# First pair: x ahead of the weights, weight conversions behind each step's work, unread products on TensorE

## The chip, the cores and the metric

One core of one Trainium2 chip. The metric is the device time of one execution in microseconds (us), a few executions per kernel. The rounds of the experiments ran on three chips, each time with the kernel before beside them (median 2079.8 to 2081.2 us). A time is about 1.8 us more than the span of the same execution in its trace. Where a ratio is given with an interval, it is the mean time of one kernel's fast runs over that of the kernel before in the same rounds, so it is not quite the ratio of the medians quoted beside it; the interval is a 95% one.

In the views PE is TensorE, PEld its weight loads, DVE VectorE, ACT ScalarE, POOL GpSimd and SP SyncE; a q behind a name means its sequencer, which waits and issues. The granted clock is the share of full speed that TensorE was given. A landing is the time from a transfer's issue to the arrival of its data. The views count each product twice: three products stand as x6.

## The reference, cut to what matters

```python
x: (8, 3008, 256) f32;  w_in: (256, 2048);  w_out: (2048, 256)   # float64 in memory, read as pairs of int32
X = np.fft.fft(x, axis=1)
X = np.fft.fft(X, axis=2).real
h = X.reshape(24064, 256) @ w_in
g = h * np.clip(h + 3.0, 0.0, 6.0) / 6.0
return g @ w_out
```

The weights arrive in double precision. The kernel converts them to float32 with integer operations while the first x is being transformed.

## The kernel before: the parts concerned

Work is done in batch "pairs"; all the trouble is in the first. x comes in 8 chunks, each as a forward half and a "partner" half, the mirrored rows, which are gathered with an indirect DMA. A fold adds the two (two large operations on GpSimd, then two large and one 8-element operation on VectorE), stage 1 multiplies by the DFT table on TensorE, ScalarE copies the result to z, and z is stored.

```python
def load_x(pr, c):                                   # all on GpSimd's queue; PR = 94 rows
    nc.gpsimd.dma_start(out=xt[:, 0:n, :], in_=rows[...])                    # forward
    nc.gpsimd.indirect_dma_start(out=xr[:]..., in_=x_r, in_offset=...IX...)  # partners
...
narrow_pair(0); use_pair(0)
for c in range(NXC):                                 # window A
    fold(first, c, 0, nc.gpsimd)
    fold(first, c, 1, nc.vector)
    if c + 3 < NXC:
        load_x(first, c + 3)
    if c in (2, 5):
        narrow_pair((c + 1) // 3)                    # conversion: VectorE, ScalarE, GpSimd
    for i in range(XC // 2):
        stage1(first, c, i)
    ...load_w...; if c in (2, 5): use_pair((c + 1) // 3)
load_g(...); narrow_pair(3); stage2 ...; use_pair(3) # window B
# window C: the MLP steps; pairs 4 to 7 are converted AHEAD of steps 0, 1, 3 and 5
```

A conversion of a pair of weight blocks is 5 operations of VectorE, 3 of ScalarE and a last multiplication for each of two blocks, then 4 products and 8 small ones on TensorE (x8 and x16 in the views) for an "in" pair or sums on GpSimd for an "out" pair.

## Time and profile before

Median 2081.8 us (2078.97 to 2082.96). The span is the sum of four stretches, which are used throughout. They were read from the timeline: A ends with the last stage-1 product of the first pair, B with the first hidden s on VectorE, C with the seventh second-layer step.

| stretch, before | us | what runs in it |
|---|---|---|
| A | 84.1 | loads, 8 folds, stage 1, conversion of pairs 0 to 2 |
| B | 22.8 | z out and back in, pair 3, stage 2 |
| C | 80.2 | 7 MLP steps, pairs 4 to 7 |
| rest | 1891.5 | steady MLP, TensorE full |

The rest is TensorE-bound and untouched, so a change in the time is a change in A + B + C. The lines that carry this are in the prediction below. One view was looked at before predicting but not used as it should have been, the table of DMA issues of the first 200 us. Its columns are what is moved, queue and operation, count, size and, last, the median us from issue to landing:

```profile
xt<-in_x_dram POOLq DMA_DIRECT2D x8, 376.0 KB, 10.2
...
xt<-in_x_dram,IX POOLq DMA_INDIRECT x9, 13.8
```

A forward load takes 10.2 us to land and a gather of partners, 94 rows, 13.8 us. The prediction works with 5 us for x.

### The profile page before, as it was taken

The page shows a single profiled execution, that of the slowest core. Times are in us where ns is not written, and L with a number is a line of the kernel's source. Part 1 is how long each engine was busy: PE and PEld are TensorE (multiplying, and loading weights), DVE is VectorE, ACT ScalarE, POOL GpSimd, SP SyncE. Part 2 cuts the span into 40 slices and gives each one's busy share as a digit, 9 for nine tenths or more (in the row PEclk, how much of TensorE's full clock was granted, in tenths as well). Part 3 has the DMA queues.
Part 4 walks back from the last instruction along what each step waited for, and adds up shares of the span by engine and source line. Part 5 has one row for each costly group of instructions (what it writes and reads, how often), then busy time and mean ns, then how long its engine had stood idle before and what let it go on. Part 6 is the DMA issues. An engine that isn't in the chain of part 4 may idle for free.

```text
span 2078.6 us, 28133 instructions
## 1 busy us (share of the span) xinstructions
PE 1974.6 (95%) x9136; PEld 1692.0 (81%) x9136; DVE 1456.9 (70%) x2714; ACT 706.1 (34%) x1205; POOL 1496.1 (72%) x1662
## 2 busy tenths in 40 slices
PE   4468999999999999999999999999999999999997
PEld 1246888888888888888888888888888888888886
DVE  5366676776777677677677677677777777777775
ACT  2344333333333333333333333333333323333332
POOL 6248777877667887788667778778766766766765
PEclk7688999999999999999999999999999999999999
DMA  6420211221110122212111112211110011011000
GB/s 188 142 86 15 57 49 34 50 47 33 29 31 23 44 51 51 51 33 54 29 21 34 43 34 48 51 43 47 31 36 11 17 23 21 18 24 21 16 16 18
DMA packets 158161, 86.81 MB, mean 42 GB/s; under 512 B 132512, under 2 KB 145056, under 8 KB 158016
## 3 DMA queue, kind: packets, MB, share of 16 engines
q1 hardware_dynamic: 129856, 60.28, 12.7%
q0 software_dynamic: 28160, 24.73, 4.5%
q8 instruction: 74, 1.21, 0.3%
q14 instruction: 71, 0.58, 0.1%
HBM read 47.65 MB, written 37.22 MB: 41 GB/s over the span
## 4 chain that ended last, share of the span: by engine, by line
PE 91%; DVE 4%; DMA 2%; ACT 1%; issue 1%; POOL 1%; SPq 0%; DVEq 0%; POOLq 0%; ACTq 0%
PE acc L320 53%; PE v L266 16%; PE u L266 15%; PE ps L193 2%; PE ps L221 2%; PE wps L446 1%; PE ps L237 1%; DVE a L298 1%; DMA st<-in_moe_w_in_dram 1%; ACT t L295 1%; DVE u L279 0%; DVE ex L406 0%; DVE s L271 0%; PE wns L451 0%; DMA g<-zd 0%
## 5 line engine op out<-in xcount | busy, mean ns | idle before, releaser
L310 POOL TENSOR_TENSOR c<-a 128x512 f32<-128x512 f32 (+1 forms) x384 | 479.2, 1248 | 406.7 <-DVE a L298 258.7
L320 PE MATMUL acc<-c,G 128*128 128x256 f32 (+1 forms) x3072 | 714.1, 375 | 0.0
L320 PEld LDWEIGHTS acc<-c,G 128*128 128x128 f32 x3072 | 579.3, 191 | 73.8 <-POOL c L310 0.2
L295 ACT ACTIVATE t<-u,half 128x512 f32<-128x512 f32 (+2 forms) x416 | 272.3, 655 | 1074.8 <-DVE u L279 1063.2
L271 DVE SCALAR_TENSOR_TENSOR s<-qn,WN,u 128x256 f32<-128x256 f32 x768 | 334.4, 477 | 392.2 <-PE u L266 391.9
L320 PE MATMUL acc<-a,G 128*128 128x256 f32 (+1 forms) x2304 | 553.6, 377 | 0.0
L320 PEld LDWEIGHTS acc<-a,G 128*128 128x128 f32 x2304 | 436.8, 191 | 57.3
L266 PE MATMUL v<-q,W 128*128 128x256 f32 x1536 | 398.8, 382 | 17.9 <-DVE a L298 17.9
L266 PE MATMUL u<-q,W 128*128 128x256 f32 x1536 | 394.5, 379 | 0.0
L266 PEld LDWEIGHTS v<-q,W 128*128 128x128 f32 x1536 | 291.3, 191 | 64.3 <-issue 21.9
L266 PEld LDWEIGHTS u<-q,W 128*128 128x128 f32 x1536 | 287.4, 190 | 65.3 <-issue 20.9
L298 DVE SCALAR_TENSOR_TENSOR a<-t,u 128x512 f32<-128x512 f32 (+2 forms) x416 | 265.9, 646 | 105.3 <-ACT t L295 101.0
L310 POOL TENSOR_TENSOR c<-a,c 128x256 f32<-128x256 f32 (+1 forms) x384 | 275.0, 716 | 30.1
L310 POOL TENSOR_TENSOR c<-c,a 128x256 f32<-128x256 f32 (+1 forms) x384 | 275.0, 716 | 30.1
L279 DVE TENSOR_TENSOR u<-s,v 128x512 f32<-128x512 f32 (+1 forms) x384 | 263.0, 685 | 42.6 <-PE v L266 2.5
L295 ACT ACTIVATE t<-v,half 128x512 f32<-128x512 f32 (+1 forms) x384 | 257.0, 669 | 5.3 <-DVE v L285 4.4
L285 DVE TENSOR_TENSOR v<-v,s 128x512 f32<-128x512 f32 (+1 forms) x384 | 257.7, 671 | 1.1
L298 DVE SCALAR_TENSOR_TENSOR a<-t,v 128x512 f32<-128x512 f32 (+1 forms) x416 | 255.1, 619 | 0.1
L310 POOL TENSOR_TENSOR r<-w,e 128x256 f32<-128x256 f32 (+1 forms) x96 | 92.3, 982 | 3.8
L193 PE MATMUL ps<-y,F 94*96 94x512 f32 x120 | 67.0, 656 | 26.2 <-DVE y L159 20.1
L326 ACT ACTIVATE e<-acc 128x512 f32<-128x512 f32 (+1 forms) x192 | 87.0, 543 | 2.9 <-PE acc L320 2.8
L346 DVE STREAM_TRANSPOSE o<-r 128x256 f32<-128x256 f32 (+1 forms) x192 | 72.4, 415 | 6.5 <-POOL r L310 6.4
(70 smaller groups left out, 826.7 us busy)
## 6 DMA issues: line engine op xcount, KB each, us to landing
out_dram<-o SPq DMA_DIRECT2D x736, 32.0 KB, 1.6
zd<-z SPq DMA_DIRECT2D x32, 384.0 KB, 3.0
g<-zd SPq DMA_DIRECT2D x48, 256.0 KB, 4.2
xt<-in_x_dram POOLq DMA_DIRECT2D x28, 376.0 KB, 3.9
st<-in_moe_w_in_dram SPq DMA_DIRECT2D x8, 512.0 KB, 4.4
st<-in_moe_w_out_dram SPq DMA_DIRECT2D x8, 512.0 KB, 5.7
T<-in_c_stage_dram SPq DMA_DIRECT2D x12, 128.0 KB, 7.2
xt<-in_x_dram POOLq DMA_DIRECT2D x4, 282.0 KB, 3.4
```

Source lines behind the costliest of these rows:

```text
L193: nc.tensor.matmul(ps[0:PZ], F[0:PR, 0:PZ], y[:, 2 * i:2 * i + 2, :], start=True, stop=True)
L221: nc.tensor.matmul(ps[:, blk, 2 * u:2 * u + 2], g[:, kk, blk * P:(blk + 1) * P], T[:, :, gr, blk, kk], start=True, stop=True)
L266: nc.tensor.matmul(ps[:, i], W1[:, blk, f * P:(f + 1) * P], q[:, blk, of:of + KC], start=True, stop=True)
L271: nc.vector.scalar_tensor_tensor(s[:, i].rearrange("p k n -> p (k n)"), qn[:, of * N2:(of + KC) * N2], WN[:, f:f + 1], u[:, i].rearrange(" ...
L279: nc.vector.tensor_tensor(u[:, :, 0:ns], s[:, :, 0:ns], v[:, :, 0:ns], op=AL.add)
L285: nc.vector.tensor_tensor(v[:, :, 0:nm], v[:, :, 0:nm], s[:, :, 0:nm], op=AL.subtract)
L295: nc.scalar.activation(t, h, AF.Relu, bias=half[:], scale=scale)
L298: nc.vector.scalar_tensor_tensor(dst, t, 1.0, h, op0=AL.min, op1=AL.mult)
L310: nc.gpsimd.tensor_tensor(out, in0, in1, op=AL.add)
L320: nc.tensor.matmul(ch.acc[i // 2][:, i % 2, 0:ch.n], G[:, i, fc, :], mv, start=(fc == 0 and i % 2 == 0), stop=(fc == NF - 1), skip_group_c ...
L326: nc.scalar.mul(ch.e[:, k:i + 1, 0:ch.n], ch.acc[i // 2][:, 0:i + 1 - k, 0:ch.n], 1.0 / WS)
L346: nc.vector.transpose(o[:, 0:n // DH, h], ch.r[:, m, h, 0:n].rearrange("p (j i) -> p j i", i=DH))
```

## The change

Its intent: get x and the folds through without a weight conversion between them; convert pairs 1 to 7 later, behind work that TensorE already has; fill TensorE's waits for x with products that nobody reads, to keep its clock up (granted clock 0.71 in A and 0.64 in B before). The core of the diff, cut:

```diff
+        nr, eng = (PR + 2, nc.sync) if pr.p == 0 else (PR, nc.gpsimd)     # forward x: 96 rows, SyncE
+        eng.dma_start(out=xt[0:nr, 0:n, :], in_=rows[...])
...
-        eng = nc.vector if j < 6 else nc.gpsimd          # last multiplication of a conversion
+        eng = nc.vector if j < 2 else nc.gpsimd
...
-        nc.scalar.mul(g[5], g[5], -1.0)                  # sign moved into finish()
...
     narrow_pair(0)
+    keep_awake(8)                                        # unread 128x128x512 products
     use_pair(0)
     for c in range(NXC):
         fold(first, c, 0, nc.gpsimd)
+        if c + 3 < NXC:
+            load_partners(first, c + 3)                  # gather, still 94 rows, GpSimd
         fold(first, c, 1, nc.vector)
-        if c + 3 < NXC:
-            load_x(first, c + 3)
-        if c in (2, 5):
-            narrow_pair((c + 1) // 3)
         for i in range(XC // 2):
             stage1(first, c, i)
+        if c + 3 < NXC:
+            load_forward(first, c + 3)
+        keep_awake(3)
...
+    narrow_pair(1); use_pair(1); keep_awake(5)
     load_g(first, 0); load_g(first, 1); load_t(1)
-    narrow_pair(3)
+    narrow_pair(2); use_pair(2)
     stage2 ...
-    use_pair(3)
...                                                      # MLP steps: pairs 3 to 7
-            for i, t in enumerate((0, 1, 3, 5)):         # ahead of step t
+            for i, t in enumerate((0, 1, 1, 3, 4)):      # behind step t
```

More of the change, by code (lines that the diff above doesn't have):

```diff
@@ L47 @@
 NK1 = (N1 + 1) // 2
-PROD = ("P1", "P2", "-P4", "P5", "P7", "P6", "P3")
+PROD = ("P1", "P2", "-P4", "P5", "P7", "-P6", "P3")
 @with_exitstack
@@ L116, in __init__ @@
             self.p = p
-            self.x, self.y, self.z = {}, {}, {}
+            self.x, self.xr, self.y, self.z = {}, {}, {}, {}
             self.zd = None
@@ L125, in x_tile, with load_forward, load_partners @@
             pool, tag = ((apool, "a"), (cpool, "c"), (spool, "t"))[(i >= 8) + (i >= 11)]
-        return pool.tile([PR, XC, D], F32, tag=tag, name="xt")
+        return pool.tile([PR + 2, XC, D], F32, tag=tag, name="xt")
     def load_x(pr, c):
-        xt, xr = x_tile(pr, 2 * c), x_tile(pr, 2 * c + 1)
-        rows = x_pn[pr.p * PR:(pr.p + 1) * PR]
+        load_forward(pr, c)
+        load_partners(pr, c)
+    def load_forward(pr, c):
+        xt = x_tile(pr, 2 * c)
+        nr, eng = (PR + 2, nc.sync) if pr.p == 0 else (PR, nc.gpsimd)
+        rows = x_pn[pr.p * PR:pr.p * PR + nr]
         n = XC if c < NXC - 1 else XC - 1
-        nc.gpsimd.dma_start(out=xt[:, 0:n, :], in_=rows[:, c * XC + 1:c * XC + 1 + n, :])
+        eng.dma_start(out=xt[0:nr, 0:n, :], in_=rows[:, c * XC + 1:c * XC + 1 + n, :])
         if n < XC:
-            nc.gpsimd.dma_start(out=xt[:, n:XC, :], in_=rows[:, 0:1, :])
+            eng.dma_start(out=xt[0:nr, n:XC, :], in_=rows[:, 0:1, :])
+        pr.x[c] = xt
+    def load_partners(pr, c):
+        xr = x_tile(pr, 2 * c + 1)
+        pr.xr[c] = xr
         i = pr.p * NXC + c
         nc.gpsimd.indirect_dma_start(
-            out=xr[:].rearrange("p n d -> p (n d)"), out_offset=None, in_=x_r,
+            out=xr[0:PR].rearrange("p n d -> p (n d)"), out_offset=None, in_=x_r,
             in_offset=bass.IndirectOffsetOnAxis(ap=IX[:, i:i + 1], axis=0),
         )
-        pr.x[c] = xt, xr
     def fold(pr, c, part, eng):
-        xt, xr = pr.x[c]
+        xt, xr = pr.x[c][0:PR], pr.xr[c][0:PR]
         n = XC if c < NXC - 1 else XC - 1
@@ L165, in fold @@
             eng.tensor_copy(y[:, n, 0:P + 1:P], xt[:, n, 0:P + 1:P])
-        del pr.x[c]
+        del pr.x[c], pr.xr[c]
     starting = [True]
@@ L335, in finish @@
         add(rn[:, 0, 0], e[:, 0], e[:, 1])
-        add(wn[:, 0], e[:, 0], e[:, 5])
+        nc.gpsimd.tensor_tensor(wn[:, 0], e[:, 0], e[:, 5], op=AL.subtract)
         add(wn[:, 1:3], wn[:, 0:1].to_broadcast([P, 2, n]), e[:, 4:2:-1])
@@ L472, with keep_awake @@
     nc.vector.memset(ones[:], 1.0)
+    def keep_awake(n):
+        ps = ps_h.tile([P, 2 * TB], F32, tag="uv", name="awake")
+        for i in range(n):
+            nc.tensor.matmul(ps[:], ones[:], W0[:], start=True, stop=True)
+    W0 = spool.tile([P, 2 * TB], F32, tag="s", name="W0")
+    nc.vector.memset(W0[:], 0.0)
     narrow_pair(0)
+    keep_awake(8)
     use_pair(0)
@@ L476 @@
         fold(first, c, 0, nc.gpsimd)
+        if c + 3 < NXC:
+            load_partners(first, c + 3)
         fold(first, c, 1, nc.vector)
-        if c + 3 < NXC:
-            load_x(first, c + 3)
-        if c in (2, 5):
-            narrow_pair((c + 1) // 3)
         for i in range(XC // 2):
             stage1(first, c, i)
-        for j in {0: (2, 3), 2: (4,), 3: (5,), 5: (6,), 6: (7,), 7: (8, 9)}.get(c, ()):
-            load_w(j)
+        if c + 3 < NXC:
+            load_forward(first, c + 3)
+        keep_awake(3)
         if c == 4:
             load_t(0)
-        if c in (2, 5):
-            use_pair((c + 1) // 3)
+            load_w(2)
+        if c == 5:
+            load_w(3)
+            load_w(4)
+    narrow_pair(1)
+    use_pair(1)
+    keep_awake(5)
+    for j in (5, 6):
+        load_w(j)
     load_g(first, 0)
@@ L492 @@
     load_t(1)
-    narrow_pair(3)
+    narrow_pair(2)
+    use_pair(2)
+    for j in (7, 8):
+        load_w(j)
     for i in range(2):
@@ L503 @@
     NST = 2 * NF
+    after = {}
     def beside(p):
@@ L512, in beside @@
         if p == 0:
-            for i, t in enumerate((0, 1, 3, 5)):
-                for j in (10, 11, 12, 13, 14, 15)[2 * i:2 * i + 2]:
-                    put(t, load_w, j)
-                if i + 2 < NG:
-                    put(t, load_t, i + 2)
-                put(t, narrow_pair, 4 + i)
-                put(t, use_pair, 4 + i)
+            for i, t in enumerate((0, 1, 1, 3, 4)):
+                after.setdefault(t, []).extend([(narrow_pair, (3 + i,)), (use_pair, (3 + i,))])
+                for j in range(9 + 2 * i, min(11 + 2 * i, 16)):
+                    after[t].append((load_w, (j,)))
+            for gr in range(2, NG):
+                after.setdefault(gr - 1, []).append((load_t, (gr,)))
             put(NF - 1, close_w)
@@ L573 @@
         mlp2(*chunk(s))
+        for f, a in after.get(s, ()):
+            f(*a)
         if fc == NF - 1:
```

## The prediction

> **What bounds the kernel now.** I read the page's slices first, then busy time in four windows, then the chain that ended last within the first 190 us, then each engine's timeline there.
>
> ```profile
> PE   4468999999999999999999999999999999999997
> PEclk7688999999999999999999999999999999999999
> ```
>
> Each digit is 52 us. TensorE is short of work only in the first three or four slices, and the granted clock is low only there.
>
> ```profile
> 0.00:84.10 84.10, 38.15 (x88) 16.43 (x88) 46.49 (x76) 26.48 (x44) 41.17 (x41) 0.71 0.58 163
> 84.10:106.90 22.80, 11.46 (x48) 8.58 (x49) 3.33 (x7) 7.80 (x13) 3.57 (x3) 0.64 0.59 153
> 106.90:187.00 80.10, 53.95 (x199) 41.30 (x198) 53.57 (x94) 34.94 (x58) 47.71 (x52) 0.81 0.19 56
> 187.00:2078.60 1891.60, 1871.07 (x8805) 1625.69 (x8803) 1353.55 (x2538) 636.84 (x1090) 1403.65 (x1567) 1.00 0.15 34
> ```
>
> Columns: window, length, busy us of PE, PEld, DVE, ACT, POOL, clock, DMA share, GB/s. After 187.0 TensorE is busy 1871 of 1892 us; the change leaves that part alone. So the span is "end of the seventh second-layer step (186.9)" plus a constant, and the question is when that step ends. Call the three earlier windows A (x, folds, stage 1), B (way to the first hidden step) and C (first seven MLP steps, among which weights are still converted).
>
> In A, the chain of waits shows the cause:
>
> ```profile
> 24.03 0.59 ACT z L194
> 24.64 0.34 SPq L196
> 25.02 0.43 SPq L378
> 25.49 13.89 DMA st<-in_moe_w_in_dram
> ...
> 57.99 5.61 DMA st<-in_moe_w_out_dram
> ...
> 84.12 0.59 ACT z L194
> 84.72 3.00 DMA zd<-z
> 87.79 0.64 SPq L206
> 88.48 6.82 DMA g<-zd
> ```
>
> Weight loads stand between the folds: 13.9 and 5.6 us of the chain are a weight block landing, because VectorE converts it ahead of the next fold in program order, while x waits behind the same transfers:
>
> ```profile
> 31.47 1.88 POOL L139 DMA_INDIRECT xt<-in_x_dram,IX  x1 [0.30 <-issue]
> 39.78 1.50 POOL L151 TENSOR_TENSOR xt<-xt 94x508 f32<-94x508 f32 x1 [6.43 <-DMA xt<-in_x_dram,IX]
> ```
>
> In C, conversions cost TensorE 4 to 9 us each:
>
> ```profile
> 119.88 3.97 PE L446 MATMUL wps<-st,C 128*128 128x512 f32 x4 [8.62 <-POOL st L409]
> ...
> 145.47 2.05 PE L266 MATMUL v<-q,W 128*128 128x256 f32 x4 [5.88 <-DVE a L298]
> ```
>
> [...] clock 0.50 in 80:100, 1.00 later; the 128x512 product of L237 is 1.50 us in the cold chain piece (99.19) and 0.87 us in the warm one (207.84). [...] a 0.68 us conversion (L406) took 3.63 us at 44.30 beside GpSimd's folds.
>
> **The change part by part.** A: x forward moves from GpSimd's queue to SyncE's; partners stay on GpSimd, issued straight after its fold; six of eight weight loads, and pairs 1 to 3, leave the loop. GpSimd's 5.04 us per chunk (23.31 less 18.27) loses 0.6 to 0.9 of issue. In return TensorE gets 8 unread products ahead of weight pair 0, 3 after each chunk, 5 after pair 1.
>
> - The zeros are ready some 0.4 us after the ones (10.2), so at 10.6. Eight products at 1.71 cold, 0.86 warm; I estimate 3 cold (in the before, the clock rose 3.4 us after the first product) and 5 warm: 9.4, to 20.0.
> - Pair 0 on PE, warm: 4 x 0.86 + 1.7 (wns) = 5.1, to 25.2. Before it was done at 22.0, so this start is 3 us later.
> - Per chunk 2 stage-1 and 3 unread products, 5 x 0.86 = 4.3 us warm. Beside it: GpSimd 2.35 fold + 2.2 indirect issue = 4.5, but it starts at about 12 and has no partner to issue after chunk 4; x three chunks ahead needs z copy 0.7, issue 0.8, landing about 5, fold 2.35, y 1.4, stage 1 1.7 = 12 per 3 chunks, 4.0 each. So PE's 4.3 sets it, narrowly.
> - Last stage 1: 25.2 + 7 x 4.3 + 2.2 = 57.5, against 84.1. Gain 26.6.
>
> B: Before, 22.8 us. z to g still takes 11.3 (84.1 to 95.4), so g is there at 68.8. But ScalarE's order puts pair 1's conversion behind the last z copy (58.1): 4.35 for six activations (84.60 to 88.95), then 0.7 VectorE and 1.3 GpSimd, 64.6. PE's first product of it can go at 62.3; with a clock probably lost, pair 1 ends near 70.5. Unread 5: 4.3, stage 2 to 77. Pair 2's activations stand behind WN's copy (70.5): GpSimd's second product ends 7.0 later (134.28 to 141.29 in the before), G needs 3.0, then m 1.05: 81.5; ps3 and qn about 2: first hidden s at 83.5 against 106.9. B is 26.0, so 3.2 lost.
>
> C: one hidden step on VectorE is 3.7 (106.89 to 110.58). An "in" pair, from VectorE's start to wns end, is 14.7 (114.27 to 128.99). An "out" pair is 9.9 from ScalarE's start to G (134.28 to 144.2), and no longer has the sign change that held ScalarE to 144.0, worth about 1.9.
>
> - Three hidden steps, 0.8 added for a cold start: 95.4. Second-layer step 0 runs inside.
> - Pair 3: 110.1. Hidden step 3 (1.1 + 3.7): 114.9. Pair 4: 129.6. Pair 5's activations stand behind pair 4's W copies: G at 139.6; step 2 ends 143.3 cold.
> - Stage 2, hidden 5, step 3: 1.0 + 1.9 + 3.0 = 149.2. Pair 6 starts at 149.1 on VectorE, G 159.4, step 4 at 163, step 5 at 167.9. Pair 7 starts 159.3, G 169.7; GpSimd's y folds 2.75 and combine 2.75: 175.2. Step 6 ends 175.9.
>
> C is 92.4 against 80.0: one pair more (five, not four), 12.4 lost. Sum: 26.6 - 3.2 - 12.4 = 11.0 gained. 2081.8 - 11.0 = 2070.8, so 2071.
>
> **Rivals.**
> 1. *The unread products become the bound and never warm the clock.* Cold they are 1.71 each: 8.6 per chunk, stage 1 ending near 95, later than before. For: in the before the clock dropped at 25[...]. Against: the unread ones are full 128 x 128 products without gaps. It would make 2095 to 2110.
> 2. *DMA replaces the weights as the limit.* A chunk moves 0.38 MB in twice and 0.38 MB out; in 4.3 us that is 266 GB/s, while the four 20 us stretches of the before reach 109 to 190 and 80:100 reaches 211. For: that peak. Against: partners run up to three chunks ahead, and slices of the before reach 300 and more. If chunks take 5 us, A ends near 62.5 and the time is 2076.
> 3. *The gain of A is kept whole.* If B and C cost no more than before, 2055. Against: five conversions in series are counted from the program order, and each has one engine's queue behind it.
> 4. *A is eaten entirely*: with pair 1 and 2 serial and cold, C 7 us longer than I have it, 2079 to 2082.
>
> **Range and chances.** The hand count has some 40 terms, several decided by about 1 us of slack; I put plus or minus 12: 2058 to 2083, 2071 the middle. 2% is 41.6 us, which would need step 6 at 145, before my sum has even begun pair 6: 0.03. Slower by 2% needs rival 1 and more: 0.01. Within 2%: 0.96.
>
> **What would show it.** In the after: unread products of 0.86 us at clock 1.0 from about 15 on; first stage 1 at 25, last near 57, chunk spacing 4.3 with PE, not x, ending the waits; no weight load in the chain before 55. In B, PE idle on GpSimd's conversion and m, not on g. In C, PE gaps of 6 to 7 us before pairs 3 and 4 and waits on G before steps 2 and 4; PE continuous from near 176. Wrong if chunks wait for x (rival 2), if the clock reads 0.5 in 25:57 (rival 1), or if pairs 3 to 7 cost TensorE less than 12 us each over its own work.

## The result, and the profile after

Median 2089.57 us (2088.61 to 2093.95), against 2082.3 in the same rounds: ratio 1.0042, interval 1.0024 to 1.0061. That is within 2%, as given the highest chance, but above the predicted range of 2058 to 2083 and on the other side of before: the kernel lost 0.4% where 0.5% was to be gained.

The page's slices (52 us each) of the changed kernel:

```profile
PE   6768999999999999999999999999999999999997
PEclk9978999999999999999999999999999999999999
```

The unread products do what they were put in for: the first two slices were 4 4 busy at clock 7 6 and are now 6 7 at 9 9. The time did not follow. The same four stretches, as windows (columns as in the prediction):

```profile
0.00:71.70 71.70, 51.74 (x123) 22.87 (x124) 35.68 (x57) 15.55 (x25) 32.30 (x28) 0.93 0.60 172
71.70:97.80 26.10, 18.30 (x63) 10.28 (x63) 7.83 (x13) 12.81 (x22) 8.98 (x9) 0.91 0.67 186
97.80:195.40 97.60, 66.79 (x224) 44.86 (x224) 60.40 (x104) 39.33 (x64) 49.49 (x52) 0.78 0.15 46
195.40:2086.90 1891.50, 1870.94 (x8805) 1625.67 (x8803) 1354.11 (x2538) 636.77 (x1090) 1403.51 (x1569) 1.00 0.15 34
```

| stretch | before | predicted | measured | change predicted | change measured |
|---|---|---|---|---|---|
| A | 84.1 | 57.5 | 71.7 | -26.6 | -12.4 |
| B | 22.8 | 26.0 | 26.1 | +3.2 | +3.3 |
| C | 80.2 | 92.4 | 97.6 | +12.4 | +17.4 |
| sum | | | | -11.0 | +8.3 |

B is right, the rest is untouched as expected. A gave 14.2 us too little and C cost 5 us more. (The prediction took 80.0 for C of before.)

In A, the chain of waits (start, us, what) no longer has a weight landing before 61, but it has this:

```profile
2.59 8.91 DMA xt<-in_x_dram
11.54 10.59 issue
22.17 0.70 POOL xt L161
...
25.78 3.15 DVE y L169
...
43.56 6.95 DMA xt<-in_x_dram
...
51.46 3.14 DVE y L169
```

x itself is the first thing on the chain; then comes a stretch of 10.6 us for which the chain names nobody. GpSimd's timeline (start, us, engine, line, operation, and in brackets the idle time before it and its releaser) names it:

```profile
3.84 1.69 POOL L150 DMA_INDIRECT xt<-in_x_dram,IX  x1 [3.39 <-DVE IX L473]
...
22.17 1.25 POOL L161 TENSOR_TENSOR xt<-xt 94x508 f32<-94x508 f32 x1 [12.94 <-DMA xt<-in_x_dram,IX]
...
42.48 1.25 POOL L161 TENSOR_TENSOR xt<-xt 94x508 f32<-94x508 f32 x1 [7.13 <-DMA xt<-in_x_dram]
...
59.25 1.26 POOL L161 TENSOR_TENSOR xt<-xt 94x508 f32<-94x508 f32 x1 [4.70 <-DMA xt<-in_x_dram,IX]
```

The gather issued at 3.84 holds the first fold until 22.17; the prediction had the folds begin at about 12. And from the fold of chunk 0 at 22.17 to that of chunk 3 at 42.48 are 20.3 us, for three chunks. What ends the wait at 42.48 is not a gather (a gather carries IX) but the forward load. SyncE issues it only behind the store of chunk 0's z:

```profile
33.35 0.32 SPq L206 DMA_DIRECT2D zd<-z  x1
33.71 0.44 SPq L141 DMA_DIRECT2D xt<-in_x_dram  x1
```

By the semaphore times in the trace, chunk 3's gather had landed at 37.8 and its forward load landed at 42.3, 8.6 us after its issue. The forward load also came last for chunks 4 and 7, the gather for chunk 6 (the fold at 59.25). The view of the tile over the same stretch, with the count, then the least, median and greatest duration in ns, and its last line, which here holds the gathers alone, gives two more numbers:

```profile
L169 DVE TENSOR_TENSOR y<-xt x8: 161/166/3220, 25.7 to 67.9; 94x8 f32<-94x8 f32 x7, 94x6 f32<-94x6 f32 x1
...
DMA to landing us min/median/max: 12.4/15.8/18.3
```

A gather lands after a median of 15.8 us. And an operation on 8 elements, 0.17 us in the median, takes 3.2 us three times (two of them on the chain, at 25.78 and 51.46). So two suspects for A: the landing of x, gathers and the forward loads beside them, and something that holds VectorE. For C, two more: five conversions in series, and the clock (0.78 against 0.81 before).

### The profile page after: what moved, and what is told of

It is laid out like the page before. It is cut to its first block, busy times and chain, and to the rows that moved or that the text cites. A ratio compares the mean times of both kernels' runs of the same rounds, so it can differ in the third digit from the quotient of the medians.

```text
span 2086.9 us, 28289 instructions
## 1 busy us (share of the span) xinstructions
PE 2007.8 (96%) x9210; PEld 1703.7 (82%) x9210; DVE 1458.0 (70%) x2711; ACT 704.5 (34%) x1201; POOL 1494.3 (72%) x1657
## 4 chain that ended last, share of the span: by engine, by line
PE 90%; DVE 3%; issue 2%; ACT 2%; POOL 1%; DMA 1%; SPq 0%; DVEq 0%; POOLq 0%; ACTq 0%
PE acc L330 52%; PE v L276 15%; PE u L276 15%; PE ps L203 2%; PE ps L231 2%; PE ps L247 1%; DMA xt<-in_x_dram 1%; PE wps L455 1%; DVE a L308 1%; PE awake L486 1%; POOL st L419 0%; ACT t L305 0%; DVE u L289 0%; DVE s L281 0%; DVE y L169 0%
```

## The experiments

Theory going in: the landing of the 94-row gathers spaces the loop; everything else in the prediction's A is right. Rivals: the unread products bound or cost something; the moved x loads were the harm; moving conversions only moves their time.

Every version gave correct results. Stretches are from the one profiled execution of each; times are of four executions.

### 1. The gather over 96 rows

```diff
-            out=xr[0:PR].rearrange("p n d -> p (n d)"), ...     # 94 rows, IX of 94 rows
+            out=xr[:].rearrange("p n d -> p (n d)"), ...        # 96 rows; two are never read
```

> The changed kernel with the gather of the partners over 96 rows instead of 94 (two rows more, unread). Theory X[...] (a 94-row gather[...] 4 KB packets of 0.16 us at 7 to 13 per us for one gather):[...] the gather lands in 5 to 8 us instead of 13 to 18, the first fold starts near 14 instead of 22, chunk spacing falls to 4.3 to 5 us, A ends near 58 to 62, total 2075 to 2081. Rival L (a gather's time is fixed[...]): landing stays 13 to 18 us, total within 2 us of the changed kernel.

Measured: 2076.96 us, ratio 0.9986 (0.9969 to 1.0002), against 1.0042 for the change as it was. First stage-1 product at 25.8 (25.2 predicted), spacing 4.3 us (4.3), A 58.6 (57.5), B 28.9, C 96.5. The last line of the same view of the tile, in which forward loads are counted too (the gathers alone have a median of 5.0 as well):

```profile
DMA to landing us min/median/max: 4.2/5.0/14.3
```

and the DMA queues in the first 24 us, first of the change, then of this version (packets, MB, share of 16 engines):

```profile
DMA packets 3313, 3.85 MB, mean 160 GB/s; under 512 B 2135, under 2 KB 2391, under 8 KB 3313
...
q0 software_dynamic: 2304, 1.16, 19.3%
```

```profile
DMA packets 1470, 4.32 MB, mean 180 GB/s; under 512 B 176, under 2 KB 432, under 8 KB 1470
...
q0 software_dynamic: 462, 1.63, 28.8%
```

More data goes in a fifth of the packets on GpSimd's queue; some two thousand packets of under 512 bytes are gone. These are packets of 4 bytes (2022 against 64); the rows go in packets of 4096 bytes in both versions. What differs for the rows is how many packets move at once, by the packet records of the two traces: while one 94-row gather was in flight, 2 for nearly all of the time that any moved, and with three in flight mostly 4 to 6; with 96 rows, up to 16 or 17 for one. The forward loads of the loop changed as well, though their edit is the same: they landed in 4.2 to 5.6 us, against 6.0 to 8.6 beside the 94-row gathers.

With two rows more, A becomes what was predicted. That the 94-row gathers are the cause is shown, but not by their own landing alone: they also slow the forward loads, and how they do that is not shown. The chain shows that TensorE, not x, now sets the loop: stage 1 and unread products alternate without a gap.

```profile
25.93 1.80 PE ps L203 x4
27.73 2.58 PE awake L486 x6
30.30 1.72 PE ps L203 x4
32.02 2.58 PE awake L486 x6
```

The same edit in the kernel before, without the change:

> The kernel before with one thing changed: the gather of the partners covers 96 rows instead of 94. Theory G (the 94-row gather[...] is what x waits for): first fold from 18.3 to about 15, A ends a few us earlier where the chain waits for x, but most of A's chain there is weight landings (13.9 and 5.6 us), which lie on SyncE's queue: gain 3 to 8 us, total 2072 to 2077. Rival W (weight landings alone bound A, x is hidden): no change within 2 us.

2076.2 us, ratio 0.9979 (0.9962 to 0.9995): A 81.1, B 22.7, C 80.0. So the edit is worth some 4 us of the medians there (2080.04 in the same rounds) and about 12.6 in the changed kernel, which depends on the gather more; but with it, both kernels take the same time. The chain of this one still has weight landings of 10.31 and 5.59 us in A.

### 2. Without the unread products

```diff
-    keep_awake(8) ... keep_awake(3) ... keep_awake(5)
```

> The changed kernel without any of its 37 unread products. Theory X (x limits window A: the partners' landing of 13 to 18 us and the forward load queued behind the z store set the chunk spacing): the products filled idle time only, so first stage 1 comes earlier or the same, the clock reads 0.5 over most of A, each stage-1 pair costs 3.4 instead of 1.7 us; the total moves by less than 6 us from the changed kernel's 2089, either way. Rival P (the unread products themselves hold up stage 1[...]): A ends 5 to 10 us earlier and the total is 2080 to 2084.

2094.47 us, 1.0065 (1.0048 to 1.0082), A 73.1, B 28.1, C 102.2. The rival is out: without the unread products the median is 5 us higher, not lower. The same on top of the 96-row gather, where they fill the chain:

> The 96-row gather in the changed kernel, and none of the 37 unread products. With the fast gather the chain of A was 32% unread products (chunk spacing 4.3 = 5 x 0.86). Theory K (they are now the bound, and TensorE's half clock would cost less): first stage 1 near 22, chunk spacing 3.5 to 4.2, A ends 50 to 54; B and C somewhat longer by lost clock (2 to 6 us); total 2070 to 2077. Rival H (the clock is worth more than the products cost, as in the 94-row case, where leaving them out cost 5 us): total 2079 to 2083.

2081.89 us, 1.0009 (0.9992 to 1.0026): A 59.9 instead of 58.6, C 101.7 instead of 96.5. All four of its times lie above all four of the version with them. Even where they are a quarter of the chain of the first 100 us they cost nothing: without them the last fold starts at 52.0 us instead of 50.4, as folds wait 5.77 and 5.52 us for x.

Where the 5 us lie is not shown. C is longer here, but over all versions with this order of conversions it falls into two groups: 94.8 to 97.6 us at a granted clock of 0.78 to 0.82, and 101.4 to 102.2 us at 0.73 to 0.75. Two versions that keep unread products, that of experiment 3 and the first of experiment 7, are in the second group too. One profile of C thus says little about an edit.

### 3. x loads as before

> The changed kernel with x loaded as before (forward rows on GpSimd's queue, 94 of them, issued with the partner after VectorE's part); weights, conversions and unread products as changed. If the x move gives anything by itself (theory X1), A ends later than 71.7 by 3 to 8 us and the total is 2092 to 2098. Rival: the x move costs (forward loads wait for z's store on SyncE, and VectorE's small fold op is caught behind GpSimd's next fold for 3.2 us at three chunks): A ends 3 to 8 us earlier and the total is 2081 to 2086.

2085.65 us, 1.0026 (1.0009 to 1.0043); A 69.7, against 71.7 with the move. The move of x to SyncE, one of the change's headings, gave A nothing in this profile.

### 4. Conversions in their old places, the rest of the change kept

> The changed kernel with the weight loads and conversions put back where they were before (pairs 1 and 2 in the x loop, 3 ahead of stage 2, 4 to 7 ahead of their steps); x and the unread products stay as changed. Theory S (the loss is the series of five conversions after A: B and C cost 3.3 and 17.5 us more): B and C fall back by some 15 to 20 us; A may grow by a few us because weight loads and VectorE conversions return to it. Total 2070 to 2080. Rival D (conversions cost the same wherever they stand, since DMA for the weights and x share the queue): A grows by as much as C falls, total 2085 to 2092.

2087.68 us, 1.0031 (1.0014 to 1.0047). Columns of the windows as before:

```profile
0.00:95.20 95.20, 60.91 (x147) 27.25 (x148) 47.83 (x77) 25.95 (x43) 36.08 (x32) 0.84 0.52 146
95.20:118.10 22.90, 18.31 (x64) 11.22 (x64) 3.19 (x6) 7.80 (x13) 3.58 (x3) 0.85 0.58 144
118.10:195.20 77.10, 52.62 (x200) 39.66 (x199) 57.31 (x94) 33.78 (x55) 46.75 (x50) 0.82 0.20 58
```

A grows by 23.5, B and C shrink by 3.2 and 20.5: the seventh step ends at 195.2 instead of 195.4. In this kernel, with its 94-row gathers, the places of the conversions make no difference to the sum. With the 96-row gather as well:

> 96-row gather, x and unread products as changed, weight loads and conversions where they were before. Theory V (in the x loop, conversions cost A what they save in C because VectorE waits in order for a weight block that lands late, 11.5 and 9.4 us of that chain): A falls from 95 only by the gather's part, to 85 to 90, B 23, C 77: total 2077 to 2083. Rival (the slow gather also slowed the weight blocks[...]): A below 80, total 2065 to 2073.

2079.8 us, 1.0001 (0.9985 to 1.0018): 80.8, 22.9, 77.1. The profiled execution was the fastest of its four (2074.08). The median is 2.8 us above that of experiment 1, and the intervals overlap.

### 5. The conversions of C behind instead of ahead, alone

From the last version, one thing changed:

```diff
-                put(t, narrow_pair, 4 + i); put(t, use_pair, 4 + i)
+                after.setdefault(t, []).extend([(narrow_pair, (4 + i,)), (use_pair, (4 + i,))])
```

> The kernel with the conversions in their old windows and the 96-row gather, in which only one thing is changed: pairs 4 to 7 are converted behind the work of steps 0, 1, 3 and 5 instead of ahead of it. C was 77.1 us there. If converting behind a step's work is what the change is good for, C falls by 3 to 10 us. If the order within a step is worth nothing because the conversions follow each other in series anyway, C stays within 2 us; if a later conversion just comes later, C grows by up to 5.

C was 84.0, so 6.9 longer than in the fastest execution of the last version; 2082.55 us, 1.0007 (0.9991 to 1.0024), where the version with "ahead" had 1.0001 in other rounds. "Behind each step's work" bought nothing here.

### 6. All x first

The first attempt at a better version: 96-row gather, x of six chunks queued first, pairs 0 to 2 converted between the chunks.

> A version built from what the runs say: 96-row gather, x of the first six chunks queued before anything else but the stage-1 table, C and weights between and behind, pairs 0 to 2 converted in the x loop after chunks 1, 3 and 5, pair 3 and the rest as before, 4 unread products at the start and 1 after each chunk. Expected from bytes: 7.6 MB by about 31 us, chunk spacing 3 to 5 with three conversions between, A 50 to 62, B 23, C 77 to 80: total 2045 to 2060. If conversions in order again hold x up (theory V in full), A is over 75 and the total over 2070.

A miss: 2076.88 us, 0.9991 (0.9974 to 1.0007), A 87.3. The rival of its expectation came true, conversions hold x up: GpSimd's last two folds stand behind pair 2's conversion, which it began at 69.61 after 36.45 us of waiting. And VectorE's timeline has one integer operation of a conversion taking 9.51 us at 23.93, where the others take 0.42, while GpSimd ran four folds back to back. The second attempt kept the conversions where the change puts them:

```diff
  ... (cut: the loop's own loads move from c + 3 to c + 6 with it)
-    for c in range(3):            # x queued at the start
+    for c in range(6):
-        keep_awake(3)
+        keep_awake(1)
```

> The changed kernel with the gather over 96 rows, with x of six chunks queued at the start instead of three, and with 1 unread product per chunk instead of 3 (8 and 5 elsewhere as before). If nothing but the landing of x and the unread products holds the loop once the gather is quick, its first stage-1 product stays at 25 to 26 us, the spacing falls from 4.3 us to about 3 us, window A ends at 46 to 50 us, B stays 27 to 29, C 96 to 98, and the time is 2066 to 2070 us (0.992 to 0.995 of before). Rival: GpSimd's back-to-back folds hold VectorE's small operations, as seen in the front-loaded version, so that A stays at 55 to 59 and the time at 2075 to 2078.

2075.81 us, 0.9981 (0.9962 to 1.0); first stage 1 at 25.0, A 57.5. The rival was right. VectorE's and GpSimd's timelines:

```profile
25.14 11.64 DVE L169 TENSOR_TENSOR y<-xt 94x8 f32<-94x8 f32 x1
36.70 0.67 DVE L167 TENSOR_TENSOR y<-xt 94x508 f32<-94x508 f32 x1
```

```profile
25.41 1.28 POOL L161 TENSOR_TENSOR xt<-xt 94x508 f32<-94x508 f32 x1
...
35.67 1.07 POOL L162 TENSOR_TENSOR xt<-xt 94x508 f32<-94x508 f32 x1
```

With x there, GpSimd runs five folds, ten operations, in one go from 25.41 to 36.74, and VectorE's 8-element operation, which began at 25.14, ends with them at 36.78. It is the second suspect again, at over three times the size. Is it the small operation that suffers?

> The same with the 8-element operation of VectorE's fold put ahead of its two large ones. If it is the small operation alone that suffers from GpSimd's next fold, A ends 3 to 8 us earlier than in the version without this edit. If whichever operation runs when GpSimd's next fold begins is held, the long duration only moves to another of the three, and A and the time stay within 1 us of it.

With the small operation put ahead of its two large ones: 2075.82 us, 0.9975 (0.9958 to 0.9991), A 57.7. It was again the small operation that was held, for 10.78 us from 26.98, until GpSimd's last fold ended at 37.72. So its place among VectorE's operations is not the cause. That it need not be the small one is seen in the first attempt, where an integer operation was held for 9.51 us, and in experiment 1, where a large operation of chunk 0 took 3.15 us instead of 0.68. What the held operations have in common is that GpSimd ran folds beside them, and each ended with the last of the row or up to 0.6 us after it.

> The six-chunk version with the conversion of pair 2 put behind stage 2 and the Nyquist sum instead of ahead of them. If pair 2's conversion is on the path of window B, B falls from about 28 to 20-22 us and part of it (the wait of the first second-layer product for pair 2) comes back in C, which grows by 4 to 8; time 0 to 4 us better. If the conversions are zero-sum, B falls and C grows by the same, and the time is within 1 us.

With pair 2's conversion put behind stage 2: B 27.6, C 100.2, 2076.99 us, 0.9978 (0.9962 to 0.9995). B gained 2.0 and C lost 5.4 in the profiled execution, its slowest, and the ratio is the same, so again nothing.

### 7. The folds off GpSimd

```diff
-        fold(first, c, 0, nc.gpsimd)
+        fold(first, c, 0, nc.vector)
```

On the six-chunk version:

> The six-chunk version (96-row gather, 1 unread product per chunk) with the first pair's large folds on VectorE instead of GpSimd. If GpSimd's folds hold VectorE, then with all four large operations on VectorE at about 0.7 us each a chunk takes about 3 us, the long operations of 10 us vanish, the first stage-1 product stays at 22 to 25, A falls from 57.5 to 46-51 and the time from 2075.8 to 2066-2071. Rival: with the folds off GpSimd, PE at half clock or the landing of the last x (45.9 us before) holds A at 55 or more, and the time stays.

2064.71 us, 0.9924 (0.9907 to 0.9941); A 45.9. Four large operations on VectorE now take about 0.68 us each and none is held:

```profile
28.73 0.68 DVE L161 TENSOR_TENSOR xt<-xt 94x508 f32<-94x508 f32 x1
29.33 0.68 DVE L162 TENSOR_TENSOR xt<-xt 94x508 f32<-94x508 f32 x1
30.11 0.68 DVE L167 TENSOR_TENSOR y<-xt 94x508 f32<-94x508 f32 x1
30.71 0.68 DVE L168 TENSOR_TENSOR y<-xt 94x508 f32<-94x508 f32 x1
31.31 0.16 DVE L169 TENSOR_TENSOR y<-xt 94x8 f32<-94x8 f32 x1
```

The first two were 1.28 and 1.07 us on GpSimd, in the lines above. The other engine was not only in the way; it was also slower at the work, and this run does not separate the two. The median falls by 11.1 us, with rounds on two chips; the ratios say much the same. On the changed kernel as it is, with its 94-row gathers:

> The changed kernel as it is, 94-row gather and all, with only the first pair's large folds on VectorE. If the landing of the 94-row gathers is what spaces its loop, as the 96-row version says, A stays within 3 us of 71.7 and the time within 3 us of 2089.6. If the holding of VectorE by GpSimd's folds is a good part of A there too, A falls by 6 or more.

2086.36 us, 1.0044 (1.0017 to 1.007). The ratio is that of the unaltered change (1.0042). Its profiled execution, the fastest of its four (2081.85 to 2094.22), has A at 64.9, which is 6.8 shorter, but the times don't bear it out; whether the hold costs time beside the slow gather stays open. Its trace shows the forward loads most clearly: with GpSimd free, the gathers of chunks 3 to 5 were issued by 13.0 and had landed by 27.2 us, yet folds 3 and 4 waited for forward loads. Those issued at 28.17 and 32.46 landed after 11.0 and 11.3 us, while two gathers were in flight; the two issued at 46.81 and 52.63, when none was, after 4.3 and 4.5 us.

> The previous version with the last multiplication of each conversion on VectorE for all pairs instead of GpSimd from pair 1 on. If the multiplications on GpSimd (1.27 us, and the hand-over to and fro) lengthen the series of conversions, B falls by 1 to 3 and C by 4 to 8 us against the previous version. If VectorE is as full as the series itself, B and C stay within 2 us.

With the multiplications of the conversions on VectorE as well: 2062.64 us, 0.9921 (0.9905 to 0.9938), B 25.6, C 94.1 instead of 28.7 and 101.4. The profiled executions promise 10 us; but the first version's was its slowest of four and the second's its fastest, and the ratios are equal. The granted clocks in the two Cs are 0.73 and 0.82, as far apart as those of the two groups in experiment 2. The multiplications on GpSimd are not shown to be the excess in C.

> The version with the conversions in their old places and the 96-row gather, with the first pair's large folds on VectorE. VectorE is then busier in A by about 2.7 us for each of 8 chunks, but isn't held by GpSimd: A 74 to 80 instead of 80.8, C as there 77 to 80, time 2074 to 2080. If the landings of the weights behind the queue's head bound A, A stays at 80 to 81.

2072.7 us, 0.9963 (0.9946 to 0.998), A 76.6, C 80.4: the old places of the conversions gain from the folds on VectorE too, less.

### 8. Is the change worth anything without its hindrances?

The kernel before with only the 96-row gather, folds and multiplications on VectorE; and the change with the same, x three chunks ahead, conversions in the old places:

> The kernel before with only three small edits: gather over 96 rows, the first pair's large folds on VectorE, all last multiplications of the conversions on VectorE. If the late landings of the second and third pair of weights still bound A, A stays at 76 to 81, C at 76 to 80, time 2068 to 2074, and the change with the same edits (2062.6) is worth about 8 us. If the two edits carry all the gain, the time comes down to 2060 to 2065 and the reordering of the change is worth nothing.

2069.12 us, 0.995 (0.9933 to 0.9967): 71.8, 22.6, 79.6.

> The change with its conversions in the old places, the 96-row gather, and folds and multiplications on VectorE. A 74 to 77, B 20 to 23, C 73 to 78; time 2066 to 2070 if the places of the conversions cost A what its weights' landings cost there, 2060 to 2063 if conversions are zero-sum as in the changed kernel.

2074.34 us, 0.9971 (0.9954 to 0.9988): 76.0, 23.2, 80.8. That is 5.2 us of the medians above the kernel before with the same edits, in the same rounds: with x three chunks ahead and the conversions in the old places, the rest of the change (x on SyncE, unread products) costs time.

| version | us | ratio to before | A | B | C |
|---|---|---|---|---|---|
| the change | 2089.57 | 1.0042 | 71.7 | 26.1 | 97.6 |
| + 96-row gather | 2076.96 | 0.9986 | 58.6 | 28.9 | 96.5 |
| + six chunks ahead, fewer unread | 2075.81 | 0.9981 | 57.5 | 29.6 | 94.8 |
| + folds on VectorE | 2064.71 | 0.9924 | 45.9 | 28.7 | 101.4 |
| + multiplications on VectorE | 2062.64 | 0.9921 | 46.1 | 25.6 | 94.1 |
| before + 96 rows, folds, multiplications | 2069.12 | 0.995 | 71.8 | 22.6 | 79.6 |

The best version beats both kernels, and beats the kernel before with the same three edits by 6.5 us of the medians, in different rounds (the intervals of the ratios overlap slightly). It differs from that kernel in the places of the conversions, the rest of the change, x six chunks ahead and fewer unread products; no run separates these.

## Why the prediction was wrong

**The step that failed** is in part A: "x three chunks ahead needs z copy 0.7, issue 0.8, landing about 5, fold 2.35, y 1.4, stage 1 1.7 = 12 per 3 chunks, 4.0 each. So PE's 4.3 sets it, narrowly." The term of the sum that was mis-sized most is the landing. It was put at 5; the forward loads of the loop took 8.6, 8.4, 7.0, 8.1 and 6.0 us, and the partners, which were taken to run ahead on their own, 12.4 to 18.3. From fold 0 to fold 3 the sum was: fold 2.3, y 4.4, stage 1 to the issue of the forward load 4.7, landing 8.6. That is 20.0 of the 20.3 us measured, where 2.35, 1.4, 3.2 and 5 had been put. So 3.6 us are the landing, 3.0 the held operation in y, and 1.5 stage 1, which took 3.7 us after TensorE had waited 4.0. From fold 3 to fold 6 (16.8 us) the gather came last: it was issued 2.5 us after fold 3 began and landed after 14.2. The landing failed at the start too: "it starts at about 12" was 22.2, and had been 18.27 in the kernel before. Together: first stage 1 at 29.0 instead of 25.2 (3.8), seven spacings of 5.77 instead of 4.3 (10.3), which is the 14.2 us missing in A. The proof is the first experiment: two rows more in the gather, forward loads and gathers landing in about 5 us in the loop, and A is 58.6. Two held operations (3.15 and 3.06 us) are left in it, but they end by 25.9 us, when TensorE has just finished pair 0.

The numbers were at hand: 10.2 us for a forward load and 13.8 for a gather stood in the view of the DMA issues of before. As an estimate, with 10.2 in place of 5 in the prediction's own sum three chunks take 17.2 us, 5.7 each; A would have come out at 25.2 + 40.1 + 2.2 = 67.5 and the time near 2081. What the rows have to do with it was first shown by experiment 1: by the packet records of the two traces, 2 packets moved at a time for one 94-row gather, up to 16 or 17 with 96 rows.

**The second hidden wait.** The prediction has an example of a VectorE operation held beside GpSimd's folds, 3.63 us instead of 0.68, but gives the hold no term in A. In the changed kernel it is on the chain with 3.15 and 3.14 us. In a loop that has its x, with six chunks ahead, A stays at 57.5 with it; with the folds on VectorE, A is 45.9 and the time falls 11.1 us; how much of that is the hold, and how much the faster fold, is not separated. With six chunks ahead the operation was held for 11.64 us, until five folds in a row had ended.

**B** was right to 0.1 us, by its own steps: TensorE waits on GpSimd's conversion (2.29 us before the first product of pair 1) and on m (4.40 us), not on g. Some of that is luck: m was done 1.8 us sooner after A's end than predicted, and the last leg to the first hidden s took 3.9 us instead of 2; and with the 96-row gather B was 28.9.

**C** was right in mechanism, with five conversions in series and TensorE waiting 6.87 and 5.45 us ahead of the "in" pairs, and 5 us too short:

```profile
116.39 3.78 PE L455 MATMUL wps<-st,C 128*128 128x512 f32 x4 [6.87 <-POOL st L419]
...
135.76 4.08 PE L455 MATMUL wps<-st,C 128*128 128x512 f32 x4 [5.45 <-POOL st L419]
```

Pair 3 took 15.9 us where 14.7 was put, pair 4 took 16.8 and pair 7 12.7 instead of 10.4: 5.6 in all. The timelines show where. Pair 3 lost 1.3 us ahead of its first product on TensorE, which began 6.9 us after VectorE's start instead of 5.6. Pair 4 lost 1.8 in its second two products (3.78 us, where the same two of the pair in the kernel before, and of pair 3, took 1.98). In pair 7 the first four operations of VectorE took 4.1 us, against 1.8 in pair 6. The trace of another execution would give other sizes: see the two groups of C in experiment 2.

**The rivals.** The first, unread products as the bound, is refuted by taking them out (5 us slower). The second, DMA as the limit, was right that chunks would come late and wrong about the cause: it counts GB/s, and asks for 266, but the change moved 172 in A with x late, and the 96-row version 212 with x in time. The third, that A's gain is kept whole, is out: B and C cost 20.7 us more. The fourth, A eaten by B and C, is right about the exchange, which was 23.5 against 23.7 when the conversions were put back, and about C, which was 5 us longer than in the sum. Of the three signs of an error that the prediction names, "Wrong if chunks wait for x" is the one that came true (the clock in 25 to 57 was 0.87). And the unread products themselves went as written: 10.86 to 19.7, pair 0 done at 25.0.

## What to carry to other kernels

Before counting a loop that depends on transfers, take the landing time of each of its transfers from the profile, each by its own issue and beside what else is in flight, and ask of each wait which of them came last; a bandwidth (172 GB/s in A here) said nothing about one gather over 94 rows, which landed after a median of 15.8 us, nor about the load beside it (6.0 to 8.6 us). Work that is moved from one serial stretch to the next is not saved: look for what the two stretches can do at once. And when two engines share folds, try giving all of them to the faster one (here VectorE, 0.68 us an operation against 1.07 to 1.28 on GpSimd) before ordering them more cleverly.
